# A recurrent-attention and feed-forward kernel: inputs laid out transposed, states on quarters of the array, and a four-operation weight decode on three engines

## Chip, cores, metric

One core of one Trainium2 chip. The metric is the device time of one execution in microseconds (us), by the slowest core; here there is one. A run is classed slow when it is over 1.5% above the fastest of the same kernel.

## The reference

For 4 batches, 8 heads, 768 tokens and 64 features per head, a decayed state is carried from token to token; the 3072 x 512 result goes through a feed-forward layer with an ELU:

```python
for t in range(S):
    state = gamma * state + outer(k[:, :, t], v[:, :, t])     # per head, 64 x 64
    y[:, :, t] = scale * (q[:, :, t] @ state)
x = y.transpose(0, 2, 1, 3).reshape(B * S, H * D)             # 3072 x 512
h = x @ w_in                                                  # 512 x 2048
g = where(h > 0, h, exp(min(h, 0)) - 1)
out = g @ w_out                                               # 2048 x 512
```

q, k, v are fp32. The weights arrive as float64: their bits are loaded and rounded to fp32 on the chip ("decode"), 32 pieces of 128 x 512.

## The kernel before

Tokens are taken in 24 chunks of 128, six to a batch. A chunk's q and k are scaled, transposed on TensorE and copied out of PSUM; scores, masked scores times v, and q times the state follow. Four chunks make a block of the feed-forward part, whose 32 steps (16 for `hp`, 16 for `op`, each 8 matmul records) run among the next block's chunks. A scheduler orders the instructions. The parts that matter here, with cuts:

```python
def decode(upto):                                # ten VectorE operations a piece
    ...
        vec.tensor_scalar(pw, hi, 20, 0x7FF, ALU.logical_shift_right, ALU.bitwise_and)
        vec.tensor_scalar(pw, pw, 896.0, 1151.0, ALU.max, ALU.min)
        vec.tensor_scalar(pw, pw, 896.0, 2.0**23, ALU.subtract, ALU.mult)
        vec.scalar_tensor_tensor(pw, hi, 0x80000000, pw, ALU.bitwise_and, ALU.bitwise_or)
        ...                                      # six more, of which three with two tensor inputs
def turn(m):                                     # scale q and k, transpose two heads at a time
    ...
    nc.tensor.transpose(tp[:, p, :], src[:, 2 * p : 2 * p + 2, :], ident)
    ...
def values(m, state):
    ...
    for p in range(HP):
        for hh in range(2):                      # half of the array's columns each
            nc.tensor.matmul(y[hh * D : (hh + 1) * D, p, :], lhsT=vn[:, 2 * p + hh, :], rhs=pt[:, hh, p, :], ...)
        if i > 0:                                # whole array, a pair of states on the diagonal
            nc.tensor.matmul(y[:, p, :], lhsT=state[1][:, p, :], rhs=qT[:, p, :], start=False, stop=True)
```

Of the kernel before, what the change touches and what calls it, by code (L numbers as in the profile page):

```python
# [10 lines left out]
I32 = mybir.dt.int32  # L11
# [6 lines left out]
def kernel(  # L18
    ctx: ExitStack,
    tc: tile.TileContext,  # L20
    q: bass.AP,
    k: bass.AP,
    v: bass.AP,
    moe_w_in: bass.AP,
    moe_w_out: bass.AP,
    out: bass.AP,
):
    # Retention in its chunked form, C tokens at a time, all in fp32.  With the
    # token's place i in its chunk, q is scaled by gamma^i / sqrt(D) and k by
    # gamma^-i, so that the masked scores hold gamma^(t-s).  The state  # L30
    #   T <- gamma^C (T + k'^T v)
    # carries the earlier chunks, decayed to the start of the present one.
    # The outputs come out transposed (features on partitions), which is the
    # layout that the first product of the feed-forward part takes.
    #
    # The weights come in as float64, for which the engines have no type: their bits
    # are loaded, and each is rounded to fp32 here, once (see decode).
# [4 lines left out]
    B, H, S, D = q.shape  # L42
    DM, DFF = moe_w_in.shape
    NTOK = B * S
    C = P  # tokens in a chunk
    TB = 512  # tokens in a block of the feed-forward part
    HP = H // 2  # pairs of heads; a pair fills the 128 partitions
# [6 lines left out]
    NW = 4  # parts of a sum over DFF  # L54
    assert D == 64 and DM == H * D and KJ == HP and S % C == 0 and NTOK % TB == 0
    assert NFT % NW == 0 and DFF % 512 == 0 and DM == 512
    scale = 1.0 / math.sqrt(D)
    gammas = [1.0 - 2.0 ** (-5.0 - h) for h in range(H)]

    const = ctx.enter_context(tc.tile_pool(name="const", bufs=1))  # L60
    ldpool = ctx.enter_context(tc.tile_pool(name="ldpool", bufs=2))
    wraw = ctx.enter_context(tc.tile_pool(name="wraw", bufs=4))
    scaled = ctx.enter_context(tc.tile_pool(name="scaled", bufs=2))
    tpool = ctx.enter_context(tc.tile_pool(name="tpool", bufs=2))
# [6 lines left out]
    ps_t = ctx.enter_context(tc.tile_pool(name="ps_t", bufs=2, space=PSUM))  # L71
    ps_s = ctx.enter_context(tc.tile_pool(name="ps_s", bufs=2, space=PSUM))
    ps_y = ctx.enter_context(tc.tile_pool(name="ps_y", bufs=1, space=PSUM))
    ps_c = ctx.enter_context(tc.tile_pool(name="ps_c", bufs=1, space=PSUM))
    ps_f = ctx.enter_context(tc.tile_pool(name="ps_f", bufs=2, space=PSUM))

# [4 lines left out]
    def load(m):  # L81
        if m >= NCHUNK:
            return
        b, i = chunks[m]
        got = []
        for name, src, bufs in (("qn", q, 3), ("kn", k, 3), ("vn", v, 5)):
            t = ldpool.tile([C, H, D], FP32, name=name, tag=name, bufs=bufs)
            nc.sync.dma_start(t, src[b, :, i * C : (i + 1) * C, :].rearrange("h s d -> s h d"))  # L88
            got.append(t)
        raw[m] = got  # L90

    # Weights in pieces of 128 rows by 512 columns, w_in's in the order in which
    # ffn() comes to them, then w_out's.
    WC = 512
    FPC = WC // P
    w_in_sb = [
        [const.tile([P, WC], FP32, name=f"w_in{n}_{j}") for j in range(KJ)] for n in range(DFF // WC)
    ]
    w_out_sb = [const.tile([P, DM], FP32, name=f"w_out{f}") for f in range(NFT)]
    pieces = [  # L100
        (moe_w_in[j * P : (j + 1) * P, n * WC : (n + 1) * WC], w_in_sb[n][j])
        for n in range(DFF // WC) for j in range(KJ)
    ]
    N_IN = len(pieces)
    pieces += [(moe_w_out[f * P : (f + 1) * P, :], w_out_sb[f]) for f in range(NFT)]
    staged, decoded = [], []

    def load_piece():
        if len(staged) < len(pieces):
            src, dst = pieces[len(staged)]  # L110
            # low and high words of each float64, as they lie in memory
            t = wraw.tile([P, WC, 2], U32, name="wraw", tag="wraw")
            nc.sync.dma_start(t.rearrange("p c w -> p (c w)"), src.bitcast(U32))
            staged.append(t)

    def decode(upto):
        """Round pieces to fp32: (1 + m 2^-52) 2^(e - 1023), m's top 23 bits and the rest
        summed in fp32, e held to fp32's range (0 below it, inf above)."""
        vec = nc.vector
        while len(decoded) < upto:  # L120
            t, dst = staged[len(decoded)], pieces[len(decoded)][1]
            lo, hi = t[:, :, 0], t[:, :, 1]
            pw, m = dst.bitcast(U32), hi.bitcast(FP32)
            vec.tensor_scalar(pw, hi, 20, 0x7FF, ALU.logical_shift_right, ALU.bitwise_and)
            vec.tensor_scalar(pw, pw, 896.0, 1151.0, ALU.max, ALU.min)
            vec.tensor_scalar(pw, pw, 896.0, 2.0**23, ALU.subtract, ALU.mult)
            vec.scalar_tensor_tensor(pw, hi, 0x80000000, pw, ALU.bitwise_and, ALU.bitwise_or)  # L127
            vec.tensor_scalar(hi, hi, 3, 0x007FFFF8, ALU.logical_shift_left, ALU.bitwise_and)  # L128
            vec.scalar_tensor_tensor(hi, lo, 29, hi, ALU.logical_shift_right, ALU.bitwise_or)  # L129
            vec.tensor_scalar(lo, lo, 0x1FFFFFFF, None, ALU.bitwise_and)  # L130
            vec.scalar_tensor_tensor(m, lo, 2.0**-29, hi, ALU.mult, ALU.add)  # L131
            vec.tensor_scalar(m, m, 2.0**-23, 1.0, ALU.mult, ALU.add)  # L132
            vec.tensor_tensor(out=dst, in0=m, in1=dst, op=ALU.mult)  # L133
            decoded.append(dst)
            load_piece()

    LEAD = 3
    for m in range(LEAD):
        load(m)
    for _ in range(4):  # L140
        load_piece()

# [1 line left out]
    ident = const.tile([P, P], FP32, name="ident")  # L144
    make_identity(nc, ident)
    # cmask[s, t] = 1 where t >= s
# [5 lines left out]
    pos_i = const.tile([P, H], I32, name="pos_i")  # L152
    nc.gpsimd.iota(pos_i, pattern=[[0, H]], base=0, channel_multiplier=1)
# [3 lines left out]
    expo = const.tile([P, H], FP32, name="expo")  # L157
    nc.vector.tensor_copy(expo, pos_i)
    nc.vector.tensor_tensor(out=expo, in0=expo, in1=lng, op=ALU.mult)
    qf = const.tile([P, H], FP32, name="qf")  # L160
    nc.scalar.activation(qf, expo, AF.Exp)
    nc.vector.tensor_scalar_mul(qf, qf, scale)
    kf = const.tile([P, H], FP32, name="kf")
    nc.scalar.activation(kf, expo, AF.Exp, scale=-1.0)
    # gamma^C: of the partition's own head, and zero for the other head of the pair
    gc = const.tile([P, HP], FP32, name="gc")
    gc2 = const.tile([P, HP, 2], FP32, name="gc2")
    nc.vector.memset(gc2, 0.0)
    for p in range(HP):
        for hh in range(2):  # L170
            r = slice(hh * D, (hh + 1) * D)
            nc.vector.memset(gc[r, p : p + 1], gammas[2 * p + hh] ** C)
            nc.vector.memset(gc2[r, p, hh : hh + 1], gammas[2 * p + hh] ** C)

# [1 line left out]
    act, xts = {}, {}  # L176

    def turn(m):
        """Scale q and k of a chunk and transpose them, two heads at a time."""
        qn, kn, vn = raw.pop(m)  # L180
        qs = scaled.tile([C, H, D], FP32, name="qs", tag="qs", bufs=1)
        nc.vector.tensor_tensor(out=qs, in0=qn, in1=qf.unsqueeze(2).to_broadcast([C, H, D]), op=ALU.mult)  # L182
        ks = scaled.tile([C, H, D], FP32, name="ks", tag="ks")
        nc.gpsimd.tensor_tensor(out=ks, in0=kn, in1=kf.unsqueeze(2).to_broadcast([C, H, D]), op=ALU.mult)  # L184
        turned = []
        for name, src in (("qT", qs), ("kT", ks)):
            tp = ps_t.tile([P, HP, C], FP32, name="tp", tag="tp")
            for p in range(HP):
                nc.tensor.transpose(tp[:, p, :], src[:, 2 * p : 2 * p + 2, :], ident)  # L189
            t = tpool.tile([P, HP, C], FP32, name=name, tag=name)  # L190
            nc.scalar.copy(t, tp)
            turned.append(t)
        act[m] = dict(ks=ks, vn=vn, qT=turned[0], kT=turned[1])

    def scores(m):
        """pt[s, hh, p, t]: the masked scores of head 2p+hh, keys on partitions."""
        a = act[m]
        sc = [ps_s.tile([C, HP, C], FP32, name="sc", tag="sc") for _ in range(2)]
        for p in range(HP):
            for hh in range(2):  # L200
                r = slice(hh * D, (hh + 1) * D)
                nc.tensor.matmul(sc[hh][:, p, :], lhsT=a["kT"][r, p, :], rhs=a["qT"][r, p, :], start=True, stop=True)  # L202
        pt = ppool.tile([C, 2, HP, C], FP32, name="pt", tag="pt")
        for hh in range(2):
            nc.vector.tensor_tensor(  # L205
                out=pt[:, hh], in0=sc[hh], in1=cmask.unsqueeze(1).to_broadcast([C, HP, C]), op=ALU.mult
            )
        a["pt"] = pt

    def values(m, state):  # L210
# [5 lines left out]
        if c == 0:  # L216
            xts[tb] = xpool.tile([P, KJ, TB], FP32, name="xt", tag="xt")
# [133 lines left out]
```

## Time and profile before

| | before |
|---|---|
| median of the runs | 892.7 us (891.2 to 893.7, 4 runs) |
| profiled span | 890.9 us |
| first feed-forward record (`hp`) | 82.1 us |
| first record of the second product (`op`) | 185.9 us |
| from there to the end | 705.0 us |

In the slices a digit is the busy share of an engine in a fortieth of the span, in tenths (9 is 90% or more); PEclk is the clock granted to TensorE, in tenths of full speed. The chain is the work that ended last, followed back from the end of the run to what released each step. In a timeline the columns are start and length in us, engine, line, operation, output and inputs, shapes and count; consecutive instructions of one group on one engine are merged. What a group costs is read from start to next start, as lengths overlap. The lines themselves stand in the prediction.

### The profile page before, as it was taken

What the parts mean: (1) busy time and instruction counts of PE and PEld (TensorE: products, weight loads), DVE (VectorE), ACT (ScalarE), POOL (GpSimd) and SP (SyncE); (2) the same over time, 40 slices, a digit from 0 to 9 for tenths busy, and PEclk for the clock granted to TensorE, in tenths of its full rate; (3) what the DMA queues carried; (4) which work ended last, traced back from release to release, by engine and by line L of the source; (5) the groups of instructions that cost most, each with busy time, mean ns of one, the idle gap of its engine ahead of it and who ended that gap; (6) DMA issues with size and microseconds to landing.
All of it is one profiled execution on the core that took longest, in us unless ns stands there. A gap on an engine that the chain in (4) does not pass through costs nothing.

```text
span 890.9 us, 7518 instructions
## 1 busy us (share of the span) xinstructions
PE 824.1 (93%) x2976; PEld 403.5 (45%) x2976; DVE 368.8 (41%) x676; ACT 146.9 (16%) x267; POOL 89.1 (10%) x77
## 2 busy tenths in 40 slices
PE   4177787899999999999999999999999999999997
PEld 3054343444454454454444444444544544444443
DVE  5999999890044421034511134411244400134200
ACT  2010211210023310023300033300033300033100
POOL 2822201000010011000001100001100000000000
PEclk9556998799999999999999999999999999999999
DMA  9755423302011021011011021011000000000000
GB/s 236 181 157 154 117 83 111 99 20 60 12 48 36 1 59 48 13 35 36 2 47 48 14 58 36 1 35 36 24 0 1 1 12 13 24 1 0 1 24 24
DMA packets 81442, 42.42 MB, mean 48 GB/s; under 512 B 75776, under 2 KB 75776, under 8 KB 81408
## 3 DMA queue, kind: packets, MB, share of 16 engines
q1 hardware_dynamic: 79488, 35.66, 15.6%
q0 software_dynamic: 1920, 6.29, 1.8%
q8 instruction: 23, 0.38, 0.2%
q14 instruction: 11, 0.09, 0.0%
HBM read 35.65 MB, written 6.29 MB: 47 GB/s over the span
## 4 chain that ended last, share of the span: by engine, by line
PE 64%; issue 17%; DVE 16%; SPq 1%; DMA 1%; POOL 0%; ACT 0%; POOLq 0%; ACTq 0%
PE op L286 28%; PE hp L268 26%; PE y L235 3%; PE y L230 3%; PE sc L202 2%; DVE wraw L131 2%; DVE wraw L129 2%; PE tp L189 2%; DVE w_in L127 1%; DVE wraw L130 1%; DVE wraw L128 1%; DVE wraw L132 1%; SPq L88 1%; DVE w_in L133 1%; PE kv L224 1%
## 5 line engine op out<-in xcount | busy, mean ns | idle before, releaser
L268 PE MATMUL hp<-xt,w_in 128*128 128x512 f32 x768 | 342.6, 605 | 5.9 <-ACT r L276 5.1
L286 PE MATMUL op<-w_out,g 128*128 128x512 f32 x768 | 334.1, 593 | 1.0 <-ACT r L276 1.0
L268 PEld LDWEIGHTS hp<-xt,w_in 128*128 128x128 f32 x768 | 146.8, 194 | 185.9 <-issue 175.2
L286 PEld LDWEIGHTS op<-w_out,g 128*128 128x128 f32 x768 | 144.3, 190 | 176.4 <-issue 173.6
L293 DVE COPY ot<-op 128x512 f32<-128x512 f32 x24 | 16.6, 691 | 301.7 <-PE op L286 301.7
L279 DVE SCALAR_TENSOR_TENSOR g<-e,r 128x512 f32<-128x512 f32 x96 | 72.2, 752 | 86.0 <-ACT e L277 86.0
L274 DVE TENSOR_SCALAR e<-hp 128x512 f32<-128x512 f32 x96 | 66.1, 689 | 94.7 <-PE hp L268 94.7
L276 ACT ACTIVATE r<-hp 128x512 f32<-128x512 f32 x96 | 57.4, 598 | 272.3 <-DVE e L274 272.3
L184 POOL TENSOR_TENSOR ks<-kn,kf 128x512 f32<-128x512 f32 x24 | 44.2, 1845 | 318.5 <-issue 258.3
L230 PE MATMUL y<-pt,vn 128*64 128x128 f32 x384 | 46.1, 317 | 31.0 <-DVE pt L205 28.0
L236 ACT COPY xt<-y 128x512 f32<-128x512 f32 x24 | 14.1, 586 | 368.2 <-PE y L235 320.1
L277 ACT ACTIVATE e<-e 128x512 f32<-128x512 f32 x96 | 59.8, 623 | 0.0
L295 POOL DMA_DIRECT2D out_dram<-ot x24 | 13.7, 570 | 340.9 <-DVE ot L293 340.9
L235 PE MATMUL y<-qT,diag 128*128 128x128 f32 x160 | 44.6, 366 | 0.0
L247 POOL TENSOR_TENSOR diag<-total,gc 128x512 f32<-128x512 f32 x20 | 30.7, 1534 | 138.4 <-DVE total L245 86.7
L230 PEld LDWEIGHTS y<-pt,vn 128*64 128x64 f32 x384 | 22.4, 148 | 47.1 <-issue 38.9
L202 PEld LDWEIGHTS sc<-qT,kT 64*128 64x128 f32 x384 | 28.6, 204 | 16.4 <-issue 13.3
L235 PEld LDWEIGHTS y<-qT,diag 128*128 128x128 f32 x160 | 27.5, 216 | 16.4 <-issue 15.8
L205 DVE TENSOR_TENSOR pt<-sc,cmask 128x512 f32<-128x512 f32 x48 | 32.0, 684 | 6.9 <-PE sc L202 6.9
L202 PE MATMUL sc<-qT,kT 64*128 64x128 f32 x384 | 34.4, 305 | 0.0
L224 PE MATMUL kv<-vn,ks 128*64 128x64 f32 x320 | 15.0, 238 | 20.0 <-DVE total L245 10.7
L182 DVE TENSOR_TENSOR qs<-qn,qf 128x512 f32<-128x512 f32 x24 | 17.7, 737 | 24.8 <-PE tp L189 20.9
(44 smaller groups left out, 299.3 us busy)
## 6 DMA issues: line engine op xcount, KB each, us to landing
wraw<-in_moe_w_in_dram SPq DMA_DIRECT2D x16, 512.0 KB, 4.7
wraw<-in_moe_w_out_dram SPq DMA_DIRECT2D x16, 512.0 KB, 3.3
qn<-in_q_dram SPq DMA_DIRECT2D x24, 256.0 KB, 3.3
kn<-in_k_dram SPq DMA_DIRECT2D x24, 256.0 KB, 3.6
vn<-in_v_dram SPq DMA_DIRECT2D x24, 256.0 KB, 3.5
out_dram<-ot POOLq DMA_DIRECT2D x24, 256.0 KB, 2.3
```

The costliest lines, as they stand in the source:

```text
L184: nc.gpsimd.tensor_tensor(out=ks, in0=kn, in1=kf.unsqueeze(2).to_broadcast([C, H, D]), op=ALU.mult)
L202: nc.tensor.matmul(sc[hh][:, p, :], lhsT=a["kT"][r, p, :], rhs=a["qT"][r, p, :], start=True, stop=True)
L205: nc.vector.tensor_tensor(out=pt[:, hh], in0=sc[hh], in1=cmask.unsqueeze(1).to_broadcast([C, HP, C]), op=ALU.mult)
L230: nc.tensor.matmul(y[hh * D : (hh + 1) * D, p, :], lhsT=vn[:, 2 * p + hh, :], rhs=pt[:, hh, p, :], start=True, stop=(i == 0),)
L235: nc.tensor.matmul(y[:, p, :], lhsT=state[1][:, p, :], rhs=qT[:, p, :], start=False, stop=True)
L247: nc.gpsimd.tensor_tensor(out=diag.rearrange("p h (j d) -> p h j d", j=2), in0=total.unsqueeze(2).to_broadcast([P, HP, 2, D]), in1=gc2.uns ...
L268: nc.tensor.matmul(hp, lhsT=w_in_sb[n][j][:, f * P : (f + 1) * P], rhs=xt[:, j, :], start=(j == 0), stop=(j == KJ - 1),)
L274: nc.vector.tensor_scalar_min(e, hp, 0.0)
L276: nc.scalar.activation(r, hp, AF.Relu)
L277: nc.scalar.activation(e, e, AF.Exp)
L279: nc.vector.scalar_tensor_tensor(gt, e, -1.0, r, ALU.add, ALU.add)
L286: nc.tensor.matmul(op, lhsT=g[ft][:, c * P : (c + 1) * P], rhs=w_out_sb[ft], start=(ft == 0), stop=(ft == NFT - 1),)
```

## The change

The intent: less of what fills VectorE in the first 200 us, and less attention work on TensorE where that engine is full.

- The host lays q and k out transposed too; the eight PE transposes and their copies go. Only v is scaled (its factor carries gamma^-i); q's factor goes to the output, a VectorE product with a table as it leaves PSUM.
- The states' products run on 64 x 64 quarters of the array, all after y and kv; the diagonal copy on GpSimd goes.
- The decode has four VectorE operations, a ScalarE copy and a GpSimd integer add. Two pieces per step, beginning within the first block.
- The ELU is Exp on ScalarE, then min-and-add and a max on VectorE.
- Rows of 4 KB instead of 256 B in the loads of q, k and v; order written by hand.

```diff
-            vec.tensor_scalar(pw, hi, 20, 0x7FF, ALU.logical_shift_right, ALU.bitwise_and)
-            ...                                  # nine more on VectorE
+            nc.scalar.activation(r, lo, AF.Copy, scale=2.0**-29)
+            vec.tensor_scalar(c, hi, 0x7FFFFFFF, None, ALU.bitwise_and)
+            vec.tensor_scalar(cf, cf, 122879.9921875, 2.0**-15, ALU.min, ALU.max)
+            vec.tensor_scalar(c, c, 3, 0x3FFFFFF8, ALU.logical_shift_left, ALU.bitwise_and)
+            vec.scalar_tensor_tensor(c, hi, 0xC0000000, c, ALU.bitwise_and, ALU.bitwise_or)
+            nc.gpsimd.tensor_tensor(out=dst, in0=c, in1=r, op=ALU.add)
-                nc.tensor.transpose(tp[:, p, :], src[:, 2 * p : 2 * p + 2, :], ident)
-                nc.tensor.matmul(y[:, p, :], lhsT=state[1][:, p, :], rhs=qT[:, p, :], start=False, stop=True)
+            for u in range(2):                   # after all of y and kv
+                for a in range(2):
+                    for c in range(2):
+                        nc.tensor.matmul(y[a][c * D : (c + 1) * D, u, :], lhsT=st[r, p, :], rhs=qk[r, 0, p, :], ...)
-            nc.vector.tensor_scalar_min(e, hp, 0.0)
-            nc.scalar.activation(r, hp, AF.Relu)
-            nc.scalar.activation(e, e, AF.Exp)
-            nc.vector.scalar_tensor_tensor(gt, e, -1.0, r, ALU.add, ALU.add)
+            nc.scalar.activation(e, hp, AF.Exp)
+            nc.vector.tensor_scalar(e, e, 1.0, -1.0, ALU.min, ALU.add)
+            nc.vector.tensor_tensor(out=gt, in0=hp, in1=e, op=ALU.max)
+    ctx.enter_context(tc.manual_schedule())
+            if len(decoded) < NPIECE:            # at every feed-forward step
+                decode(len(decoded) + 2)
...                                              # loads, tables, pools and host layout cut
```

## The prediction

> **What bounds the kernel now.** I read the page's slices first, then the chain, then the timeline of one engine in two stretches. The slices (22.3 us each) show two regimes:
>
> ```profile
> PE   4177787899999999999999999999999999999997
> DVE  5999999890044421034511134411244400134200
> PEclk9556998799999999999999999999999999999999
> GB/s 236 181 157 154 117 83 111 99 20 60 12 48 36 1 59 48 13 35 36 2 47 48 14 58 36 1 35 36 24 0 1 1 12 13 24 1 0 1 24 24
> ```
>
> Until about 200 us VectorE is full and TensorE has holes (nearly none in slice 2, where its clock falls to 0.5); afterwards TensorE is full at full clock and nothing else is near its limit. The chain agrees:
>
> ```profile
> PE 64%; issue 17%; DVE 16%; SPq 1%; DMA 1%; POOL 0%; ACT 0%; POOLq 0%; ACTq 0%
> PE op L286 28%; PE hp L268 26%; PE y L235 3%; PE y L230 3%; PE sc L202 2%; DVE wraw L131 2%; DVE wraw L129 2%; PE tp L189 2%; DVE w_in L127 1%; DVE wraw L130 1%; DVE wraw L128 1%; DVE wraw L132 1%; SPq L88 1%; DVE w_in L133 1%; PE kv L224 1%
> ```
>
> The VectorE share is the weight decode (L124 to L133). Busy times overlap, so I take costs from distances between starts. TensorE's timeline in the full stretch (start, length, group):
>
> ```profile
> 278.59 0.69 PE L224 MATMUL kv<-vn,ks 128*64 128x64 f32 x16
> 279.11 0.39 PE L230 MATMUL y<-pt,vn 128*64 128x128 f32 x4
> 279.43 0.49 PE L235 MATMUL y<-qT,diag 128*128 128x128 f32 x2
> 279.85 0.44 PE L230 MATMUL y<-pt,vn 128*64 128x128 f32 x4
> ...
> 282.12 0.60 PE L189 MATMUL tp<-ident,qs 128*128 128x128 f32 x4
> 282.55 0.60 PE L189 MATMUL tp<-ident,ks 128*128 128x128 f32 x4
> 282.99 13.90 PE L268 MATMUL hp<-xt,w_in 128*128 128x512 f32 x32
> 296.82 1.16 PE L202 MATMUL sc<-qT,kT 64*128 64x128 f32 x16
> 297.91 14.00 PE L268 MATMUL hp<-xt,w_in 128*128 128x512 f32 x32
> ```
>
> One fp32 matmul is two records (a transpose one). A chunk costs kv 0.52 + y with state 3.01 + transposes 0.87 + scores 1.09 = 5.5 us. 32 feed-forward records take 13.83 or 13.93 us with the change of shape; undisturbed, their weight loads are 0.429 us apart (876.20 to 884.78 us, 20 intervals). So 1536 records are a floor of 659 us, which the change does not touch, and 24 chunks add 132: 791 us. The remaining 100 us are the slow start and about 5 us from the last matmul to the end.
>
> Two more stretches matter. A chunk without state does its y in one shape: 0.98 us for 16 records, 61 ns each, against about 109 ns for a transpose record on the whole array.
>
> ```profile
> 411.70 1.05 PE L230 MATMUL y<-pt,vn 128*64 128x128 f32 x16
> 412.68 0.66 PE L189 MATMUL tp<-ident,qs 128*128 128x128 f32 x4
> ```
>
> And GpSimd's product of 1.04 us (12.94 us in the timeline) once took 19.08 us while VectorE ran decode without a pause; it ended just after VectorE turned to `pt`, whose input is in PSUM:
>
> ```profile
> 23.04 19.08 POOL L184 TENSOR_TENSOR ks<-kn,kf 128x512 f32<-128x512 f32 x1 [7.83 <-DMA kn<-in_k_dram]
> ...
> 40.81 0.42 DVE L130 TENSOR_SCALAR wraw<-wraw 128x512 uint32<-128x512 uint32 x1
> 41.14 0.68 DVE L205 TENSOR_TENSOR pt<-sc,cmask 128x512 f32<-128x512 f32 x1
> 41.74 0.93 DVE L131 SCALAR_TENSOR_TENSOR wraw<-wraw 128x512 f32<-128x512 uint32 x1
> ```
>
> **What the Trainium skill says.** (1) "GPSIMD Engine Reference", Specifications: its SBUF interfaces are shared with VectorE, with contention when VectorE runs a 2-port mode or has two SBUF inputs. The 19.08 us agree, and so does L131 above, held to 0.93 us instead of 0.68. (2) "TensorEngine Tiling (Array Packing)", Key Properties: tiles work independently, and changing the tiling mode drains the engine. Agrees: 61 against 109 ns, and two y matmuls plus one state matmul repeat every 0.78 us where 4 x 61 + 2 x 109 ns would be 0.46. (3) "DMA: Bandwidth & Descriptors", Specifications: full rate needs at least 512 B per transfer. Agrees: 217 to 220 GB/s at 4 to 12 us with 256 B rows of q, k and v, and 381 to 414 GB/s at 15 to 18 us with weights.
>
> **The change, part by part.**
>
> *Attention on TensorE.* Removed: 8 transposes, 0.87 us. State products become 8 matmuls on quarters of the array, after y and kv, so the shape changes once rather than at each pair. y: 0.98; kv: 0.52; scores: 1.10. The 16 state records are the unknown: halves gave 61 ns at 128 columns and 32 ns at 64, so quarters should give about 33 ns, with two shape changes 0.65 us (estimate; 1.1 if only two run at once). Sum 3.35 with 0.1 for edges: 2.1 us less per chunk. With 64 feed-forward records at 27.9 us, a chunk period falls from 33.3 to 31.2 us. For the 18 or so chunks that lie in the full stretch that is 38 us.
>
> *Decode.* VectorE goes from ten operations to four: three of about 0.42 us busy that follow each other every 0.335, and one of 0.68 that holds 0.60, so 1.61 us a piece instead of six at 0.335 and four at 0.60, 4.4 us. ScalarE takes one copy (0.6 us); it was at 16%. GpSimd takes the add, about 1.04 us if an integer add costs what L184 does.
>
> *ELU.* VectorE: min-and-add from SBUF 0.335, max from PSUM 0.60. ScalarE does one Exp instead of Relu and Exp. Per step (8 records, 3.43 us of TensorE) this never binds by itself.
>
> *Start.* Whole 4 KB rows, so I count 0.4 MB per us after the first byte at 2 us. Chunk 3's data stand behind 4 chunks (1.05 MB each) and two weight pieces (0.52 MB): 5.2 MB, 15 us. Then come the scaling of v, the decode of the third piece ahead of xt on VectorE, and the y product: feed-forward starts near 21.5 us, where before it started at 82.1.
>
> *Decode phase.* 28 pieces are left, two per feed-forward step, so 14 steps. VectorE needs 0.335 + 0.60 + 2 x 1.61 = 4.15, plus 0.3 for chunk work: already above TensorE's 3.43 + 0.4. And the two adds find the port free only beside PSUM inputs or when VectorE stops; `wc` has two buffers, so VectorE must stop for them. One add shares the max (0.6 of its 1.04 hidden, 0.4 exposed), the other is exposed whole with a semaphore, 1.2. So 4.15 + 0.4 + 1.2 = 5.75, with chunk work and v's scaling 5.9 us. 14 x 5.9 = 83 us. TensorE does its 14 steps in that time.
>
> *The rest.* Steps 14 to 31 of block 0: 18 x 3.43 = 61.7, and two chunks 6.9. Blocks 1 to 4: 16 periods of 31.2 = 499. Block 5: 256 x 0.429 = 109.8. End 5. Chunks with no state or no kv (i = 0 or 5) save about 3.5 in all.
> Sum: 21.5 + 83 + 68.6 + 499 + 109.8 + 5 - 3.5 = 783.4. The timed median lies 1.4 us above the profiled span (892.3 against 890.9): **785 us**.
>
> **The rivals.**
>
> *A: the decode hides completely.* If GpSimd slips between VectorE's operations, a step costs 4.5 us and 14 cost 63: 765 us; if only TensorE bound them (3.9 us), 757. Against it: the 19 us starvation. For it: VectorE now has waits on ScalarE and GpSimd in which the port is free.
>
> *B: GpSimd becomes the bound.* If the add takes 2 us or is starved between stops, a step goes to 8 us: 14 x 8 = 112, total 814. L247's 3.03 us and L184's mean of 3.2 us over the first 178 us speak for it. Holes in TensorE could also halve its clock, as at 22 to 67 us, but a halved step (6.9 us) barely exceeds 5.9.
>
> *C: transfers bind the start.* In order on one queue, chunks 4 to 7 stand among pieces 4 to 7. At 0.4 MB per us piece 9 lands at about 36 us, with step 2, so they nearly keep up; at 0.3 the first steps slip some 8 to 10 us: 795.
>
> *D: quarters gain nothing.* State at 1.1 instead of 0.65 us adds 0.45 x 20 = 9 us: 794. In the manual order TensorE could also wait for pt or xt; but values come three steps (10 us) after scores, and the next block starts four steps after its last xt, so I expect no such wait.
>
> **Range and chances.** A and B span 757 to 814; I hold neither at its extreme, and C and D are worth under 10 us each, upward. The range is 766 to 808. Not gaining 2% (staying above 874) would need 90 us of new waits, and no rival holds more than 30. Faster 0.97, same 0.02, slower 0.01.
>
> **What would show it right or wrong.** Right: the first hp record near 21 us; hp starts some 6 us apart until about 105 us, VectorE waiting for the GpSimd add at the first decode operation, adds longer than 1.04 us; then TensorE full, 31.2 us per chunk period, state 0.65 us; no tp group. Wrong: hp steps at 3.9 us from the start (A), GpSimd busy throughout the decode (B), waits on wraw's transfers beyond 45 us (C), state over 1 us (D), or TensorE idle after 110 us, which none of the steps allows.

## The result, and the profile after

The changed kernel takes 793.4 us (792.1 to 793.5, 4 runs); its ratio to before is 0.8885 (95% interval 0.8872 to 0.8899). A ratio here compares the fast runs of both kernels of the same rounds, so it need not be the ratio of the medians above. The profiled span fell from 890.9 to 791.6 us.

The slices of the changed kernel, now 19.8 us each:

```profile
PE   6876669999999999999999999999999999999998
DVE  6999994012342001333100433100333101133000
PEclk9999898999999999999999999999999999999999
GB/s 344 325 157 211 159 187 0 80 64 17 54 8 46 67 26 67 53 1 54 66 14 80 28 26 53 45 37 67 14 1 0 3 24 14 13 1 0 14 13 26
```

The stretch in which TensorE is not full ends after slice 6 (about 119 us) instead of slice 8 (about 178 us), and nothing but TensorE is full after it. VectorE is still busy for nine tenths or more in slices 2 to 6. The chain by engine says the same, with VectorE's share at 10% instead of 16%:

```profile
PE 86%; DVE 10%; issue 2%; DMA 2%; SPq 0%; ACT 0%; ACTq 0%
```

TensorE's timeline in the full stretch, a chunk with state:

```profile
171.53 1.09 PE L212 MATMUL y<-pt,kvn 128*64 128x128 f32 x16
172.45 0.63 PE L221 MATMUL kv<-kvn 128*64 128x64 f32 x16
173.02 0.67 PE L230 MATMUL y<-qk,state 64*64 64x128 f32 x16
173.62 10.57 PE L273 MATMUL op<-w_out,g 128*128 128x512 f32 x24
...
190.98 1.16 PE L189 MATMUL sc<-qk 64*128 64x128 f32 x16
```

No `tp` group is left. y takes 0.92 us, kv 0.57, state 0.60 (173.02 to 173.62), and scores 1.09: 3.18 us a chunk instead of 5.5. From one chunk's scores to the next (190.98 to 222.02) it is 31.04 us, before 33.25.

The start, on TensorE:

```profile
22.83 1.73 PE L212 MATMUL y<-pt,kvn 128*64 128x128 f32 x16 [2.33 <-DVE xt L236]
...
27.08 7.11 PE L257 MATMUL hp<-xt,w_in 128*128 128x512 f32 x16 [0.61 <-DVE xt L236]
```

The y product of chunk 3 waited 2.33 us for VectorE's `xt`, and the first `hp` record comes at 27.1 us.

A step of the decode phase, VectorE and GpSimd (each line's bracket: idle time before it, and what ended it):

```profile
51.61 0.42 DVE L263 TENSOR_SCALAR e<-e 128x512 f32<-128x512 f32 x1
51.84 1.32 POOL L115 TENSOR_TENSOR w_in<-wc,wr 128x512 uint32<-128x512 uint32 x1 [1.62 <-DVE wc L114]
52.06 0.69 DVE L265 TENSOR_TENSOR g<-hp,e 128x512 f32<-128x512 f32 x1
52.67 0.77 DVE L110 TENSOR_SCALAR wc<-wraw 128x512 uint32<-128x512 uint32 x1
53.47 0.43 DVE L112 TENSOR_SCALAR wc<-wc 128x512 f32<-128x512 f32 x1
53.93 0.43 DVE L113 TENSOR_SCALAR wc<-wc 128x512 uint32<-128x512 uint32 x1
54.40 0.69 DVE L114 SCALAR_TENSOR_TENSOR wc<-wraw,wc 128x512 uint32<-128x512 uint32 x1
55.00 0.42 DVE L110 TENSOR_SCALAR wc<-wraw 128x512 uint32<-128x512 uint32 x1
55.23 1.31 POOL L115 TENSOR_TENSOR w_in<-wc,wr 128x512 uint32<-128x512 uint32 x1 [2.08 <-DVE wc L114]
55.46 1.37 DVE L112 TENSOR_SCALAR wc<-wc 128x512 f32<-128x512 f32 x1
56.86 0.43 DVE L113 TENSOR_SCALAR wc<-wc 128x512 uint32<-128x512 uint32 x1
57.33 0.69 DVE L114 SCALAR_TENSOR_TENSOR wc<-wraw,wc 128x512 uint32<-128x512 uint32 x1
57.93 0.42 DVE L263 TENSOR_SCALAR e<-e 128x512 f32<-128x512 f32 x1
```

From one L263 to the next it is 6.32 us. Two things are to be seen. VectorE's operations of one piece each take the result of the one before, and start 0.46 us apart. And of the two adds on GpSimd one stretches L110 to 0.77 us, the other L112 to 1.37 us; VectorE has no idle time over 0.08 us between any two operations from 31.5 to 126 us.

Where the 99.3 us of span came from, by landmarks on TensorE:

| stretch | before | after | gain |
|---|---|---|---|
| start to first `hp` | 82.1 | 27.1 | 55.0 |
| first `hp` to first `op` | 103.8 | 92.4 | 11.5 |
| first `op` to the end | 705.0 | 672.2 | 32.8 |

Some of the time after is lost to TensorE's clock. In the profile of the changed kernel the granted clock is 0.5 from 23.1 to 26.5 us, from 67.5 to 70.9, from 91.4 to 98.2 and from 118.7 to 125.5 us. The first stretch lies ahead of the first `hp`, the last one where TensorE already sets the pace: there 16 `op` records take 10.13 us, in e4, where the clock is full, 7.10.

### The profile page after: what moved, and what is told of

Read it like the earlier page. It is cut to its first block, busy times and chain, and to the rows that moved or that the text cites. A ratio compares the mean times of both kernels' runs of the same rounds, so it can differ in the third digit from the quotient of the medians.

```text
span 791.6 us, 7134 instructions
## 1 busy us (share of the span) xinstructions
PE 754.7 (95%) x2944; PEld 358.9 (45%) x2944; DVE 251.5 (32%) x484; ACT 94.3 (12%) x158; POOL 64.7 (8%) x60
## 4 chain that ended last, share of the span: by engine, by line
PE 86%; DVE 10%; issue 2%; DMA 2%; SPq 0%; ACT 0%; ACTq 0%
PE op L273 43%; PE hp L257 35%; DVE wc L112 3%; PE sc L189 3%; PE y L212 3%; DVE wc L110 2%; DVE wc L113 2%; DVE wc L114 1%; PE y L230 1%; PE kv L221 1%; DMA kvn<-in_qkv_dram 1%; DMA qk<-in_qkv_dram 1%; DVE pt L192 1%; DVE e L263 1%; DVE xt L236 0%
## 5 line engine op out<-in xcount | busy, mean ns | idle before, releaser
L263 DVE TENSOR_SCALAR e<-e 128x512 f32<-128x512 f32 x96 | 42.2, 439 | 242.6 <-ACT e L262 242.6
L262 ACT ACTIVATE e<-hp 128x512 f32<-128x512 f32 x96 | 57.1, 596 | 263.3 <-PE hp L257 263.3
L265 DVE TENSOR_TENSOR g<-hp,e 128x512 f32<-128x512 f32 x96 | 66.4, 692 | 4.0
L189 PE MATMUL sc<-qk 64*128 64x128 f32 x384 | 30.6, 298 | 6.3 <-DMA qk<-in_qkv_dram 5.7
L189 PEld LDWEIGHTS sc<-qk 64*128 64x128 f32 x384 | 25.6, 198 | 22.3 <-issue 15.2
L107 ACT ACTIVATE wr<-wraw 128x512 uint32<-128x512 uint32 x32 | 21.8, 681 | 78.5 <-POOL w_out L115 33.6
L212 PE MATMUL y<-pt,kvn 128*64 128x128 f32 x384 | 27.8, 290 | 2.3 <-DVE xt L236 2.3
L212 PEld LDWEIGHTS y<-pt,kvn 128*64 128x64 f32 x384 | 21.7, 142 | 18.2 <-issue 13.9
L112 DVE TENSOR_SCALAR wc<-wc 128x512 f32<-128x512 f32 x32 | 27.6, 863 | 1.1
L115 POOL TENSOR_TENSOR w_in<-wc,wr 128x512 uint32<-128x512 uint32 x16 | 21.5, 1344 | 48.0 <-DVE wc L114 44.2
L114 DVE SCALAR_TENSOR_TENSOR wc<-wraw,wc 128x512 uint32<-128x512 uint32 x32 | 22.2, 693 | 1.1
L110 DVE TENSOR_SCALAR wc<-wraw 128x512 uint32<-128x512 uint32 x32 | 17.0, 531 | 0.1
```

The costliest lines, as they stand in the source:

```text
L110: vec.tensor_scalar(c, hi, 0x7FFFFFFF, None, ALU.bitwise_and)
L112: vec.tensor_scalar(cf, cf, 122879.9921875, 2.0**-15, ALU.min, ALU.max)
L114: vec.scalar_tensor_tensor(c, hi, 0xC0000000, c, ALU.bitwise_and, ALU.bitwise_or)
L115: nc.gpsimd.tensor_tensor(out=dst, in0=c, in1=r, op=ALU.add)
L189: nc.tensor.matmul(sc[a][:, p, :], lhsT=qk[r, 1, p, :], rhs=qk[r, 0, p, :], start=True, stop=True)
L212: nc.tensor.matmul(y[a][c * D : (c + 1) * D, u, :], lhsT=vn[:, h, :], rhs=pt[:, a, p, :], start=(u == 0), stop=(i == 0), skip_group_check= ...
```

## The experiments

Theory 1: VectorE, with its decode, sets the time until the first `op`, and after it the chunk work on TensorE does. Theory 2, formed on the trace after: within the decode VectorE is slowed by dependence between neighbours. Rivals are named with each run. "Changed" means the kernel after the change.

| run | edit to changed | median us | ratio to before (95%) | first hp | first op | span |
|---|---|---|---|---|---|---|
| (changed) | | 793.4 | 0.8885 (0.8872, 0.8899) | 27.1 | 119.4 | 791.6 |
| e1 | ten-operation decode | 885.6 | 0.9913 (0.9894, 0.9933) | 39.3 | 211.6 | 883.6 |
| e2 | scheduler's order | 789.3 | 0.8832 (0.8818, 0.8847) | 27.4 | 117.0 | 787.0 |
| e3 | add on VectorE | 803.0 | 0.8991 (0.8977, 0.9004) | 29.5 | 130.5 | 802.3 |
| e4 | two pieces alternate | 780.2 | 0.8736 (0.8723, 0.8750) | 26.8 | 108.9 | 778.1 |
| e5 | decode over 18 steps | 786.9 | 0.8819 (0.8806, 0.8833) | 26.5 | 101.0 | 784.4 |
| e6 | rows of 256 B | 800.4 | 0.8969 (0.8954, 0.8984) | 32.7 | 129.6 | 800.5 |
| e7 | y and state alternate | 815.9 | 0.9132 (0.9097, 0.9167) | 27.7 | 121.4 | 813.3 |
| e8 | transposes put back | 808.0 | 0.9052 (0.9038, 0.9066) | 29.1 | 121.5 | 806.4 |
| e9 | no decode (wrong result) | one fast run, 756.3 | none given | 23.6 | 85.3 | 754.3 |
| e10 | e4, four steps without decode | 775.7 | 0.8695 (0.8684, 0.8707) | 26.0 | 91.5 | 773.8 |
| e11 | e10, one add of two on VectorE | 783.4 | 0.8779 (0.8768, 0.8791) | 26.0 | 100.7 | 781.4 |
| e12 | e10, min-and-add on ScalarE | 770.6 | 0.8638 (0.8626, 0.8650) | 26.7 | 90.5 | 770.6 |

All but e9 gave a correct result.

### e1: the ten operations put back

```diff
-            nc.scalar.activation(r, lo, AF.Copy, scale=2.0**-29)
-            vec.tensor_scalar(c, hi, 0x7FFFFFFF, None, ALU.bitwise_and)
-            ...
+            vec.tensor_scalar(pw, hi, 20, 0x7FF, ALU.logical_shift_right, ALU.bitwise_and)
+            ...                                  # the ten operations of before, one after the other
```

> The changed kernel with the old ten VectorE operations per weight piece put back (no ScalarE copy, no GpSimd add), all else as changed. Theory 1 (the decode on VectorE paces the first block): ten operations one after the other cost about 6 x 0.46 + 4 x 0.60 = 5.2 us a piece, a feed-forward step of two pieces 10.4 + 1.06 = 11.4 us and some chunk work instead of 6.65, so 14 steps cost some 70 us more and the four pieces of the start 12 us more: about 870 us. Rival (the gain at the start is the layout of the inputs and the order): the time stays below 815 us.

Measured 885.6 us, only 0.9% better than before. A piece takes 5.55 us (85.01 to 90.56 us in VectorE's timeline), a step without chunk work 12.17, and all of the loss, 92.2 us, has come by the first `op` (211.6 against 119.4). The rival is out: with the old decode, the new layout and the order keep almost nothing of the gain. The first `hp` does stay early (39.3 us against 82.1 before), but the first `op` comes later than before the change (211.6 against 185.9): what starts earlier is paid for in the decode phase. I had set the loss at 77 us because I took a piece as 5.2. Nor is this quite the decode of before, which let pieces alternate; see the end of the next section.

### e2: the scheduler's order

```diff
-    ctx.enter_context(tc.manual_schedule())
```

> The changed kernel without the manual order (the scheduler places the instructions). Theory 1: the order that the scheduler makes is close to the written one for the decode, so the decode phase stays as long; within 5 us of the changed kernel (787 to 798). Rival (the manual order is a large part of the gain): 810 us or more.

789.3 us: the written order is no part of the gain; it is 4 us worse than the scheduler's.

### e3: the add on VectorE

```diff
-            nc.gpsimd.tensor_tensor(out=dst, in0=c, in1=r, op=ALU.add)
+            vec.tensor_tensor(out=dst, in0=c, in1=r, op=ALU.add)
```

> The add of the decode on VectorE instead of GpSimd ([...]the last bits of the weights are wrong by about 1e-5; wrong on purpose). Theory 1: in the changed kernel an add on GpSimd holds VectorE for 0.34 us and 0.94 us in each step (1.28), and two adds on VectorE cost 2 x 0.61 = 1.22, so the step stays at 6.3 us and the time within 3 us of the changed kernel. Rival (GpSimd's add is nearly free to VectorE): a step costs 1.2 us more, 14 steps 17 us: 810 us.

The result was correct, against what I had expected: in the trace the add is one VectorE operation on 16-bit halves, 0.69 us busy. 803.0 us, 10 more than changed, so between the two expectations. VectorE's timeline:

```profile
53.35 0.69 DVE L114 SCALAR_TENSOR_TENSOR wc<-wraw,wc 128x512 uint32<-128x512 uint32 x1
54.18 0.69 DVE L115 CUSTOM_DVE_ANT_0 w_in<-wc,wr 128x1024 uint16<-128x1024 uint16 x1
54.79 0.42 DVE L110 TENSOR_SCALAR wc<-wraw 128x512 uint32<-128x512 uint32 x1
```

From L114 to L110 of the next piece it is 1.44 us, where L114 alone holds 0.60: the add costs VectorE 0.84 us, not 0.61, two of them 1.68. On GpSimd two adds held it for 0.34 + 0.94 = 1.28. The difference, 0.40, is that of the steps: 6.69 (from `hp` at 52.11 to 58.80) against 6.32. So theory 1's view holds, that the add on GpSimd is not free, with my figure for the alternative too low: moving the add to GpSimd spared VectorE only a quarter of it.

### e4: two pieces alternate

```diff
-            vec.tensor_scalar(c, hi, 0x7FFFFFFF, None, ALU.bitwise_and)
-            vec.tensor_scalar(cf, cf, 122879.9921875, 2.0**-15, ALU.min, ALU.max)
+            for j in k:                          # k: the two pieces of the step
+                vec.tensor_scalar(c[j], hi[j], 0x7FFFFFFF, None, ALU.bitwise_and)
+            for j in k:
+                vec.tensor_scalar(cf[j], cf[j], 122879.9921875, 2.0**-15, ALU.min, ALU.max)
...                                              # the same for the other two, then both adds
```

> The four VectorE operations of two pieces alternate, so that none follows the one whose result it takes. Theory 2 (dependent operations start 0.46 us apart, independent ones 0.335): six of the distances shrink by 0.125, 0.75 us a step, but without the small gaps GpSimd gets the port only when VectorE stops, so the holds do not shrink; a step of 5.6 to 6.0 us instead of 6.33, a gain of 5 to 10 us: 784 to 789 us. Rival (distance does not depend on the dependence, the holds set the pace): within 2 us of the changed kernel.

780.2 us, 13 less, somewhat more than expected. VectorE and GpSimd in a step (pairs are merged now, so x2):

```profile
47.50 3.15 POOL L123 TENSOR_TENSOR w_in<-wc,wr 128x512 uint32<-128x512 uint32 x2 [2.71 <-DVE wc L121]
48.33 0.69 DVE L274 TENSOR_TENSOR g<-hp,e 128x512 f32<-128x512 f32 x1
49.45 1.82 DVE L114 TENSOR_SCALAR wc<-wraw 128x512 uint32<-128x512 uint32 x2 [0.43 <-POOL w_in L123]
51.19 0.75 DVE L117 TENSOR_SCALAR wc<-wc 128x512 f32<-128x512 f32 x2
51.86 0.75 DVE L119 TENSOR_SCALAR wc<-wc 128x512 uint32<-128x512 uint32 x2
52.53 1.28 DVE L121 SCALAR_TENSOR_TENSOR wc<-wraw,wc 128x512 uint32<-128x512 uint32 x2
```

L117 to L119 is 0.67 us for two operations, 0.335 each, as in the kernel before, whose scheduler had alternated pieces. The step (47.87 to 53.73) is 5.86 us: 4.28 of VectorE's own, and 1.58 of waiting for the adds (0.51 ahead of L114, 1.07 within it). So the dependence was worth 0.76 a step and the holds grew by 0.30, as theory 2 had it. It saved 10.5 us of span up to the first `op`. The other 3.0 us came after it, where the work is the same: they are the stretch at half clock in the changed kernel (118.7 to 125.5 us), which e4 does not have.

### e5: the decode spread over 18 steps

```diff
-                decode(len(decoded) + 2)
+                decode(len(decoded) + 1 + (n % 2 == 0 or n == 17))
```

> The decode of two and one pieces in turn over 18 feed-forward steps instead of two in each of 14; the same instructions, and a piece is still ready before its matmul. Theory 1 (VectorE paces the first block while the second products of that block find no work in its way): VectorE's total stays, but four steps of TensorE move into it; 6 to 10 us less: 783 to 787 us. Rival (the decode phase is set by transfers or by GpSimd alone, or TensorE): within 2 us of the changed kernel.

786.9 us, as expected (6.5 less). TensorE's `op` of the first block moves to 101.0 us into time in which VectorE is still decoding `w_out`.

### e6: short rows

```diff
-        nc.sync.dma_start(qk.rearrange("p a h c -> p (a h c)"), qkv[m, :, 0:1024])
+        nc.sync.dma_start(qk... "p (b e) -> p b e", e=64, qkv[m, 0:16].rearrange("b p e -> p b e"))   # schematic
```

> The same inputs brought in rows of 256 B (the size of a row before the change) instead of 4 KB, nothing else changed. If transfers set the start, chunk 3 lands at about 25 us instead of 15 (4.2 MB at 217 GB/s plus 1 MB at 400) and feed-forward starts some 4 to 8 us later: 797 to 803 us. Rival (the start is set by VectorE, which is full from 13 us on): the first hp record within 2 us of 27.1 and the time within 3 us of the changed kernel.

800.4 us, 7 more; the first `hp` comes 5.6 us later. Between 4 and 8 us after the start the queues moved 218 GB/s instead of 382. So the layout of the rows is worth 7 us by itself, and transfers do set the start when rows are short.

### e7: y and state alternate

```diff
-        for a, u, c: y;  for p, a: kv;  for u, a, c: state
+        for p, a: kv;  for a, u: (for c: y; for c: state)    # schematic: same matmuls, other order
```

> The same 64-wide products of a chunk, but y and state alternate every two matmuls (seven shape changes more in a chunk with state). If a change of shape costs 0.1 to 0.17 us on TensorE, the group of y and state grows from about 1.5 to 2.3 to 2.7 us and 20 chunks add 14 to 24 us, less those in the decode phase where TensorE has room: 803 to 812 us. Rival (no cost for the change of shape): within 2 us of the changed kernel.

815.9 us (810.2 to 817.5), 22 more and above the expected range. TensorE, one chunk:

```profile
206.30 0.39 PE L222 MATMUL y<-pt,kvn 128*64 128x128 f32 x4
206.62 0.44 PE L229 MATMUL y<-qk,state 64*64 64x128 f32 x4
...
209.19 7.13 PE L256 MATMUL hp<-xt,w_in 128*128 128x512 f32 x16
```

y and state take 2.89 us (206.30 to 209.19) instead of 0.92 + 0.60, and the chunk period is 32.36 us instead of 31.04, 1.32 more. Within y and state the shape now changes seven times. In the changed kernel it changes once, from kv to state, so there are six changes more (not seven, as I had counted), 0.22 us each. The form before, whole-array states between the pairs, took 3.01. On quarters but alternating, the states would thus have gained almost nothing; the gain needs them after all of y. What whole-array states would cost there, no run shows.

### e8: transposes put back

```diff
+        for a in range(2):
+            for p in range(HP):                  # overwritten by the scores that follow
+                nc.tensor.transpose(sc[a][:, p, :], qk[:, a, p, :], ident)
```

> Eight transposes per chunk put back on TensorE ahead of the scores, into the PSUM tiles that the scores then overwrite (so the result stays right); nothing else. TensorE paces blocks 1 to 4 and the end of block 0: 0.87 us for eight of them plus a change of shape, some 17 or 18 chunks count: 14 to 20 us more, 807 to 813 us. Rival (they hide beside other work): within 3 us of the changed kernel.

808.0 us, 14.6 more. TensorE:

```profile
191.69 1.04 PE L191 MATMUL sc<-ident,qk 128*128 128x128 f32 x8
192.66 1.16 PE L195 MATMUL sc<-qk 64*128 64x128 f32 x16
```

0.97 us for the eight, and the chunk period is 31.91, so 0.87 more with the edges. With e7 that gives 0.87 + 1.32 = 2.19 of the 2.21 us by which the period fell. The match is closer than the method: e7 keeps the states on quarters (2.89 us), where before they were on the whole array (3.01).

### e9: no decode

```diff
+    for w in pieces:
+        nc.gpsimd.memset(w, 0.01)
...
-            ...                                  # the decode
+            vec.tensor_scalar(dst[:, 0:8].bitcast(U32), t[:, 0:8, 1], 0x3F, 0x3C000000, ALU.bitwise_and, ALU.bitwise_or)
```

> No decode: the weights are constants set by GpSimd at the start, the pieces are still brought in as before, and one tiny VectorE operation per piece frees their buffers (the result is wrong on purpose). It bounds what any better decode can give. Theory 1: feed-forward starts near 20 us, block 0 takes four periods of 31.04 us, and blocks 1 to 5 take the 607.6 us of the changed kernel: 752 to 758 us. Rival (transfers hold the first block too): 770 us or more.

The profiled run, the only fast one of four, took 756.3 us, span 754.3; the other three took 768 to 770 and are classed slow, at a granted clock of 0.999 to 1.0, which I leave unexplained. In the profile TensorE is full from 23.6 us on, at 31.04 us a period in the first block too. In this one run theory 1 holds: 37.3 us of the changed kernel's span go with the decode (791.6 less 754.3), of them 3.5 ahead of the first `hp`. By the three others it would be 24 to 25. The start is not clean either: the constants, set by GpSimd until 16.9 us, held up VectorE (a 128 x 8 operation took 3.52 us).

### e10, e11, e12: better versions

```diff
# e10: e4, and
-                decode(len(decoded) + 2)
+                decode(len(decoded) + 2 * (n % 4 != 2))
# e11: e10, and
+                (nc.gpsimd if j == 0 else vec).tensor_tensor(out=dst[j], in0=c[j], in1=r[j], op=ALU.add)
# e12: e10, and
-            nc.vector.tensor_scalar(e, e, 1.0, -1.0, ALU.min, ALU.add)
+            nc.scalar.activation(e, e, AF.Relu, scale=-1.0, bias=1.0)      # relu(1 - e)
-            nc.vector.tensor_tensor(out=gt, in0=hp, in1=e, op=ALU.max)
+            nc.vector.scalar_tensor_tensor(gt, e, -1.0, hp, ALU.mult, ALU.max)
```

> Two pieces alternate on VectorE, and four of the first 18 steps (2, 6, 10, 14) decode nothing. Theory: the gains of the two experiments add in part, 13 us for the alternation and up to 7 for the spread: 772 to 777 us, better than both kernels. Rival (one gain uses up the other): 779 to 781 us.

775.7 us: 4.5 less than e4, within the range; the gains add in part.

> As the last one, but the second piece's add is on VectorE (exact, in halves of 16 bits, 0.69 us busy and about 0.61 of distance) and the first piece's on GpSimd. Theory 1: a pair holds VectorE for 1.58 us with both adds on GpSimd; with one, the hold falls to about 0.43 beside the max and the other add costs 0.61, so a step is some 0.5 us shorter, 14 steps 7 us: 765 to 771 us. Rival (the VectorE add waits for ScalarE's copy or for the operation before it as it did alone): within 2 us of the last one.

783.4 us, 7.6 more than e10: a miss. VectorE's add takes 1.53 us instead of 0.69 (57.48 us in its timeline), because it comes while GpSimd's add of the other piece, begun at 56.88, is under way. A step is 5.95 us (58.93 to 64.88). Splitting the adds put them against each other.

> The version with alternating pieces and four steps without decode, and the min-and-add of the ELU moved from VectorE to ScalarE (relu(1 - e), with the sign turned in the max that VectorE does anyway). Theory 1 (VectorE still paces the first block): 0.46 us less in each of 18 steps, some of it taken back by GpSimd's holds, so 3 to 8 us: 768 to 773 us. Rival (the holds or GpSimd alone pace it by now): within 2 us of 775.7.

770.6 us, the best version: 5.2 less than e10, and 0.8638 of before. In its timeline VectorE stands idle for 0.57 us ahead of one L114 (56.34 us), which then takes 1.82 us for its pair instead of 0.75, so part of the 0.46 us a step was taken back by the adds.

## Why the prediction was right, and which of its terms were off

The time lay in the range: 793.4 against 785 (766 to 808). The mechanism was right in the main: VectorE with its decode paces the first block, TensorE everything after. Several terms were mis-sized, and that the sum missed by only 8.2 us of span is partly luck: 20.0 us too little for the start and the decode phase, 11.8 too much for what follows. One sign that was named for being wrong came true: TensorE still waited after 110 us (2.66 us at 112.8, 2.97 at 119.4), because the decode phase was longer.

- **Attention on TensorE**: 31.04 us a period against the 31.2 predicted, state 0.60 against 0.65; shown by the trace, and what the parts are worth (transposes 0.87, grouping by shape 1.32) by e8 and e7. Rival D, quarters that gain nothing, is out for the grouped order; in the alternating one they gain next to nothing (2.89 against 3.01).
- **Start**: first `hp` at 27.1 us, not 21.5. I took it for a matter of data (15 us) and one decode. The profile shows VectorE without a pause from about 13 to 26 us, with three decodes of 2.0 us each between the chunks' work. Without decode (e9) it is still 23.6. Of these 3.5 us 1.5 are TensorE's clock: from the y product of chunk 3 to `xt` it takes 3.68 us at half clock (from 22.83), in e9 2.20 at full clock (from 20.80). The other 2.1 I cannot place with certainty: TensorE's y waits for `xt` in e9 as well, and e9's start is not clean.
- **Decode phase, the operations**: "so 1.61 us a piece" is the step that failed. I took 0.335 us from the kernel before, where two pieces alternate, for a kernel where they don't: a piece costs 1.99, and with the min-and-add VectorE's own work in a step is 5.04 instead of 4.15 (+0.89). e4 shows it by restoring 0.335. The number was there to be read: in the trace before, the first piece's operations start at 15.77, 16.23, 16.70 and 17.16 us, 0.46 apart.
- **Decode phase, the adds**: "0.4 + 1.2" exposed; measured 0.34 + 0.94 (-0.3). The reason given for the second, that VectorE must stop for the two buffers of `wc`, is not what the trace shows: VectorE did not stop, the add began in the gap between L110 and L112 (55.23 us), and L112 took 1.37 us. Rival A (free adds) is out by these two holds and by e3. Rival B (starved, 8 us a step) did not come, and its half clock did no harm in the steps, as VectorE never waited for TensorE there. Chunk work took 0.33 us a step; the prediction named 0.3 but added only 0.15. In all, 14 steps took 93.1 us (L263 at 31.42 to 124.47), 6.65 each instead of 5.9.
- **The rest of block 0**: I put 18 steps after the decode phase, 68.6 us; it took 59.5 (124.47 to 184.02), since TensorE is already past the first `op` records when VectorE ends the phase. And I left out the 4.3 us from the first `hp` to the first L263. Predicted 173.1 us for the start of block 1, measured 184.0: +5.6 for the start, +14.4 for the decode phase, -9.1 here.
- **Blocks 1 to 5**: 607.6 against 610.3 us, as predicted; no new wait.
- **Rival C** (transfers): 409 GB/s on average from 12 to 32 us, and no loss in the changed kernel beyond the first few steps that I could find; e6 shows 7 us if rows had stayed short.

The single undoings sum to more than the gain: 92.0 (e1) + 22.4 (e7) + 14.6 (e8) + 7.0 (e6) = 136 us against 99.3. One reason offers itself: e1 pays 5.55 us for a ten-operation piece because neighbours depend on each other, where before paid 4.4 with pieces alternating; 32 x 1.15 = 37 us, about the surplus. That is argued, not shown: no run alternates the ten operations in the new kernel. The new ELU was not undone by any run either.

## What to carry to other kernels

Before an operation's distance is taken from a trace, look whether its neighbour depends on it: alternating two independent pieces was worth 13 us here for no instruction saved (3 of them through TensorE's clock). Work handed to an engine that shares a port is not gone; price it as what it holds the bound engine for (1.28 of 1.68 us here), and spread it over steps in which the bound engine has room. Group small products by shape of the array before cutting them smaller.

## What the Trainium skill lacked or had wrong

- "VectorE: DVE Perf Modes", The DRAIN you can't avoid: it says that the next operation starts when the pipe is empty, earlier if it is not held, and that a semaphore after each operation makes no difference (13.88 us either way for eight copies). It has no figure for taking the result of the operation before. Here the same kind of operation, 0.42 us busy, starts 0.335 us after an independent one and 0.46 us after one whose result it takes; e4 turned one into the other.
- "GPSIMD Engine Reference", Specifications: it names the contention with VectorE, but gives no figure for an operation on GpSimd against a train of VectorE operations. Here one of 1.04 us took 19.08 us behind operations without a gap; another got in at the gap between two dependent ones and held VectorE for 0.94 us (L112, 1.37 instead of 0.43).
- "TensorEngine Tiling (Array Packing)", Key Properties: it says that a change of mode drains the engine, without a figure. Six changes more in a chunk cost 1.32 us, 0.22 us each (e7).
